# A two-stage layer on one core: unit 0 by pairs of heads, its mixing in whole float32, and an order table in place of due times

## The chip, the cores and the metric

The kernel runs on one core of one Trainium2 chip. The metric is the device time of one execution in microseconds. The core has a matrix engine (PE, with its weight loads listed apart as PEld), three engines for elementwise work (DVE, ACT, POOL), a queue engine that issues most transfers (SP), and 16 DMA engines shared by all queues. SBUF is the on-chip memory of 128 partitions, PSUM the accumulator memory that PE writes.

## The reference

The inputs are q, k, v and a complex decay a (`a_re`, `a_im`), each of 4 batches, 8 heads, 768 steps and 48 columns, in float32, and the parameters of a gated feed-forward stage: `mu_k`, `mu_r` (384), `w_k` (384 x 1024), `w_v` (1024 x 384), `w_r` (384 x 384). For each batch and head a complex 48 x 48 state runs over the steps:

```
scale = min(|a|, 0.999) / (|a| + 1e-6)          # a scaled so that its magnitude stays under one
S     = (a * scale)[:, None] * S + k_t v_t^T    # complex S, real k v^T
y_t   = q_t @ Re(S)
```

The eight heads' y side by side are x (4 batches x 768 steps x 384 columns), and with x_prev the step before:

```
xk = mu_k * x + (1 - mu_k) * x_prev ;  xr = mu_r * x + (1 - mu_r) * x_prev
out = sigmoid(xr @ w_r) * (relu(xk @ w_k)**2 @ w_v)
```

## The kernel before

**Units.** The work is cut into 8 units: a batch and a half of its 768 steps (384 steps). Each unit goes through three phases. A *gate* phase (`gate`, lines 541 to 718) turns a, k and q into rotated keys and queries; an *attention* phase (`attend`, lines 720 to 914) makes y in chunks of 64 steps with a running state; a *mixing* phase (`mix`, lines 336 to 466) is the feed-forward stage.

**Gate.** The state's decay is written as a running sum of logarithms and of angles. ACT takes logarithms, exponentials, arctangents and sines (line 264 is the helper that issues them and loads function tables, line 261); DVE forms the running sums (scans, lines 637 and 665), clips (627, 646, 688), reduces angles (682, 685), takes an absolute value with a bit mask (691), multiplies k and q by the magnitudes (line 654, three instructions of 128 x 768 per unit) and by cosine and sine (line 704, six of them). Rows of the 384 columns lie in three tiles of 128 partitions, in the order of the heads: a head of 48 rows can lie across two tiles. Unit 0's gate is done in two groups, (0, 1) and (1, 3), of these tiles, the others' in one.

**Attention.** `stack` (line 727) copies each head's four parts, cosine and sine, key and query, by SP transfers into tiles `kq` of 112 rows, 20 transfers per unit. `advance` (755) transposes the keys on PE (768), copies them out of PSUM on ACT (774), makes the state's updates on PE (789) and adds them up on DVE (800, six additions of 112 x 384 per unit). `scores` (806) multiplies a head's 112 rows of keys and queries (818), 96 matmuls of 64 columns per unit, and DVE applies the causal mask (823). `values` (830) adds the state's part and the chunk's own part (849). ACT copies y out of PSUM into a tile `ys` (871), and 10 SP transfers per unit (882) carry it into `X`, the input of the mixing.

**Mixing.** PE multiplies in a reduced float32 form (float32r), so every operand is split into a high and a low part and every product is three matmuls: high x high, low x high, high x low (`product`, line 376). DVE makes the difference to the step before (348) and the mixed input (356); ACT rounds the high part (364), DVE subtracts for the low part (367). Nine matmuls of 128 x 384 form one block z; three blocks are the gate r, eight are `first` (line 407: z, relu on ACT 418, square on ACT 422, high part on DVE 426, low part on DVE 430) and eight are `second` (437, o, line 444). A unit's mixing is 171 matmuls. `end` multiplies r with v (460) and stores (463).

**Weights.** They arrive as 64-bit words in ten pieces (`fetch`, 483) and are converted (`convert`, 493): ACT takes an absolute value (506), DVE assembles the bits in four instructions (509, 512, 516, 520), ACT rounds the high part (526) and POOL subtracts for the low part (529). The order of the pieces is `w_r` first, then `w_k` and `w_v` in turn.

**Order.** All engines' instructions are emitted in an order that a planner in the kernel (`Plan`, lines 70 to 239) writes out before: a list schedule, with a cost for each operation, in which each engine takes, of what is ready in that model, the operation with the smallest due time (`due`, 111, worked back from the order of PE). Once emitted, every engine runs its own list in order and waits on semaphores.

## Time and profile before

| | us |
|---|---|
| median of three runs | 477.33 (476.31 to 477.69) |
| the profiled execution | 476.16 |
| its span, first to last instruction | 474.4 |
| PE busy | 382.8 |
| DVE busy | 374.5 |
| ACT busy | 299.9 |
| POOL busy | 32.3 |

Times in profile rows are microseconds from the span's start unless a row says ns. A row of a group names the line, the engine, the operation, out<-in, shapes and count, then busy time and mean ns of one, then the idle time of the engine just before these instructions and what ended it. A row of the timeline has start, length, engine, line and operation. Matmuls are pipelined and their ends are modelled, so that the distance of two starts says more about PE than the length of one. One execution was profiled; the engines not named in a wait may still have been the cause of it.

### The profile page before, as it was taken

What the parts mean: (1) busy time and instruction counts of PE and PEld (TensorE: products, weight loads), DVE (VectorE), ACT (ScalarE), POOL (GpSimd) and SP (SyncE); (2) the same over time, 40 slices, a digit from 0 to 9 for tenths busy, and PEclk for the clock granted to TensorE, in tenths of its full rate; (3) what the DMA queues carried; (4) which work ended last, traced back from release to release, by engine and by line L of the source; (5) the groups of instructions that cost most, each with busy time, mean ns of one, the idle gap of its engine ahead of it and who ended that gap; (6) DMA issues with size and microseconds to landing.
All of it is one profiled execution on the core that took longest, in us unless ns stands there. A gap on an engine that the chain in (4) does not pass through costs nothing.

```text
span 474.4 us, 12425 instructions
## 1 busy us (share of the span) xinstructions
PE 382.8 (81%) x5162; PEld 351.0 (74%) x5162; DVE 374.5 (79%) x610; ACT 299.9 (63%) x498; POOL 32.3 (7%) x45
## 2 busy tenths in 40 slices
PE   0008445879966999979989999999799988999994
PEld 0006433868755999869978898999689967999993
DVE  0798999969989889898989799569967898248222
ACT  7768445597549667957894775866669753434530
POOL 4004210214210000000000000000000000000000
PEclk9999755789978999999999999999899989999998
DMA  8998154502717056416551834072523115210101
GB/s 287 409 409 142 36 184 161 123 1 52 275 26 182 21 195 203 106 51 192 181 130 61 296 102 114 34 252 100 135 78 82 45 48 137 76 35 10 51 0 57
DMA packets 25935, 60.26 MB, mean 127 GB/s; under 512 B 5392, under 2 KB 14608, under 8 KB 25872
## 3 DMA queue, kind: packets, MB, share of 16 engines
q1 hardware_dynamic: 25872, 59.40, 40.7%
q8 instruction: 42, 0.69, 0.6%
q14 instruction: 21, 0.17, 0.1%
HBM read 31.07 MB, written 4.72 MB: 75 GB/s over the span
## 4 chain that ended last, share of the span: by engine, by line
PE 42%; DVE 28%; ACT 13%; DMA 7%; issue 5%; SPq 3%; POOL 1%; DVEq 0%; ACTq 0%
PE z L381 19%; PE o L444 12%; PE y L849 5%; DVE ph L665 4%; DMA kq<-g 3%; PE sc L818 3%; DVE g L654 3%; DMA g<-in_gat 3%; SPq L736 3%; PE up L789 2%; ACT sq L264 2%; DVE m L637 2%; DVE g L704 2%; DVE xm L356 2%; ACT L261 2%
## 5 line engine op out<-in xcount | busy, mean ns | idle before, releaser
L381 PE MATMUL z<-x,w 128*128 128x384 f32 x792 | 155.9, 347 | 5.0 <-DVE state L800 1.9
L381 PEld LDWEIGHTS z<-x,w 128*128 128x128 f32 x792 | 140.3, 193 | 8.4 <-DVE state L800 2.2
L444 PE MATMUL o<-hhi,w 128*128 128x384 f32 x384 | 103.8, 353 | 1.3 <-DVE hhi L426 1.3
L444 PEld LDWEIGHTS o<-hhi,w 128*128 128x128 f32 x384 | 71.3, 196 | 3.2 <-DVE hhi L426 2.5
L444 PE MATMUL o<-hlo,w 128*128 128x384 f32 x192 | 67.9, 354 | 5.6 <-DVE hlo L430 5.5
L768 PE MATMUL tr<-ident,g 128*128 128x128 f32 (+1 forms) x144 | 27.7, 311 | 49.3 <-DVE g L704 47.8
L418 ACT ACTIVATE r<-z 128x384 f32<-128x384 f32 x64 | 31.0, 486 | 55.2 <-PE z L381 55.0
L768 PEld LDWEIGHTS tr<-ident,g 128*128 128x128 f32 (+1 forms) x144 | 17.8, 148 | 55.9 <-issue 31.9
L426 DVE CAST hhi<-h 128x384 fp32r<-128x384 f32 x64 | 22.6, 353 | 33.3 <-ACT h L422 21.2
L704 DVE TENSOR_TENSOR g<-g,r 128x768 f32<-128x768 f32 x48 | 43.7, 951 | 1.8 <-ACT r L264 1.7
L444 PEld LDWEIGHTS o<-hlo,w 128*128 128x128 f32 x192 | 37.8, 197 | 8.7 <-DVE hlo L430 8.6
L818 PE MATMUL sc<-kq 112*64 112x64 f32 x768 | 31.7, 233 | 8.9 <-DMA kq<-g 2.7
L818 PEld LDWEIGHTS sc<-kq 112*64 112x64 f32 x768 | 26.9, 144 | 15.5 <-issue 6.2
L430 DVE TENSOR_TENSOR hlo<-h,hhi 128x384 fp32r<-128x384 f32 x64 | 35.8, 559 | 1.4
L264 ACT ACTIVATE sq<-m 128x1152 f32<-128x1152 f32 (+2 forms) x27 | 28.1, 1054 | 11.1 <-DVE m L620 7.0
L364 ACT CAST x<-xm 128x384 fp32r<-128x384 f32 x48 | 24.2, 511 | 17.1 <-DVE xm L356 13.6
L422 ACT ACTIVATE h<-r 128x384 f32<-128x384 f32 x64 | 33.2, 523 | 2.5 <-DVE hlo L430 1.5
L789 PEld LDWEIGHTS up<-v,kt 64*48 64x48 f32 (+1 forms) x1408 | 27.0, 139 | 6.8 <-ACT kt L774 3.9
L849 PE MATMUL y<-kq,state 112*48 112x64 f32 (+1 forms) x704 | 25.7, 229 | 7.5 <-DVE state L800 5.1
L849 PEld LDWEIGHTS y<-kq,state 112*48 112x48 f32 (+1 forms) x704 | 23.2, 136 | 11.4 <-DVE state L800 5.3
L789 PE MATMUL up<-v,kt 64*48 64x48 f32 (+1 forms) x1408 | 29.4, 231 | 2.4 <-DVE state L800 1.3
L529 POOL TENSOR_TENSOR w<-wx,w 128x768 fp32r<-128x768 f32 (+1 forms) x10 | 24.5, 2454 | 85.6 <-ACT w L526 85.6
(74 smaller groups left out, 551.3 us busy)
## 6 DMA issues: line engine op xcount, KB each, us to landing
kq<-g SPq DMA_DIRECT2D x96, 144.0 KB, 3.2
g<-in_gat SPq DMA_DIRECT2D x18, 768.0 KB, 6.9
raw<-in_w_all SPq DMA_DIRECT2D x9, 768.0 KB, 11.6
g<-in_gat SPq DMA_DIRECT2D x12, 384.0 KB, 7.3
v<-in_vt SPq DMA_DIRECT2D x24, 192.0 KB, 4.6
out_t<-y SPq DMA_DIRECT2D x24, 192.0 KB, 2.1
xt<-ys SPq DMA_DIRECT2D x48, 72.0 KB, 2.2
kq<-g SPq DMA_DIRECT2D x32, 96.0 KB, 2.8
```

Of the source, the lines that this page charges most:

```text
L264: nc.scalar.activation(out=out, in_=in_, func=func, **kw)
L381: nc.tensor.matmul(z, lhsT=wt[s[0]][:, part, s[1]], rhs=r[which][:, ct], start=n == 0, stop=n == 3 * NT - 1)
L418: nc.scalar.activation(out=t["r", j], in_=t["f", j], func=AF.Relu)
L422: nc.scalar.activation(out=t["h", j], in_=t["r", j], func=AF.Square)
L430: nc.vector.tensor_tensor(out=t["lo", j], in0=t["h", j], in1=t["hi", j].bitcast(F32), op=ALU.subtract)
L444: nc.tensor.matmul(tiles["o", mt], lhsT=wt[W_V + 2 * j][:, part, ts(mt, P)], rhs=r, start=j == 0 and n == 0, stop=j == NJ - 1 and n == 2)
L529: nc.gpsimd.tensor_tensor(out=t["w"][:, :, 1], in0=t["x"], in1=t["w"][:, :, 0].bitcast(F32), op=ALU.subtract)
L704: nc.vector.tensor_tensor(out=g[:, ct, 2 * i:2 * i + 2], in0=g[:, ct, 2:4], in1=t["r"][:, ct, 1 - i:2 - i].to_broadcast([P, 2, U]), op=ALU ...
L768: nc.tensor.transpose(out=t["tr", c, part][:, ct * P:(ct + 1) * P], in_=G[u][:, ct, 2 * part, c * P:c * P + rows], identity=ident)
L789: nc.tensor.matmul(t["up", c, s][i * HR:(KR if i else HR), h * D:(h + 1) * D], lhsT=keys[r, i * D:(2 * D if i else HR)], rhs=V[u][c][r, h ...
L818: nc.tensor.matmul(sc[s * SB:s * SB + SB, i, c], lhsT=kq[h][:, 0, q], rhs=kq[h][:, 1, q], start=True, stop=True)
L849: nc.tensor.matmul(t["y", v][s][rows, h // 2 % 2, c], lhsT=lhsT[:, cols], rhs=rhs, start=(s, h % 2) not in begun, stop=stop)
```

## The change

**Pair layout.** The 384 columns are put in another order on the host: tile i of 128 partitions holds the two heads of pair i in partitions 0 to 47 and 64 to 111, and in the remaining 16 + 16 partitions a third of each of heads 6 and 7. Keys of pairs 0 to 2 are read in place for the scores, as two products of 48 rows per head (cosine and sine part) in place of one of 112; heads 6 and 7 are still gathered. Queries for the state's part are copied by SP as before. ACT writes y of pairs 0 to 2 from PSUM straight into X; pair 3 goes through `ys` and six transfers.

**Unit 0 by pairs.** Unit 0's gate is done in three groups of one tile, and its attention pair by pair (`advance_pair`): transposes, updates, 24 state additions of 96 columns, scores and values of one pair need only that pair's tile. The other units work in two teams of two pairs.

**Unit 0's mixing whole.** Its inputs, hidden values and weights stay whole float32 on PE: one matmul per product in place of three, 57 in all, without the splits of lines 364, 367, 426 and 430. Its gate r comes at the end of the mixing, and `w_r` is now the last piece to be converted.

**Weights.** A piece is fetched into buffer i + 1, converted whole into buffer i, and split into buffer i - 1 once unit 0's mixing has used the piece that lies there (`split`: ACT rounds, POOL subtracts). So a conversion waits for the one before, and a split for unit 0's mixing.

**Gates.** The positive part replaces the absolute value and a separate check: one activation less per gate, with the check summed by the exponential. The absolute value of line 691 moves from DVE to ACT. For units 1 to 7, line 654's three instructions and the sine half of line 704's six move to POOL.

**Order.** A table `ORDER` gives each step of each phase a place per engine; it replaces the due times as the planner's choice among ready operations. Some of the planner's costs change, and a tile is counted free 0.16 us later.

```diff
-W_R, W_K, W_V = 0, NT, NT + 1
+W_K, W_V, W_R = 0, 1, 2 * NJ
+ORDER = {
+    ("g", 0): dict(SP=(5, 2, 7, 15, 27, 24, 9, 23, 25,), ACT=(74, 58, 34, ...
...
-R_XK = 2
+R_XK = 1
-GROUPS_0 = ((0, 1), (1, 3))
+POOL_KQ = {u: ((0,1,2), (), (0, 1, 2)) for u in range(1, NU)}
+GROUPS_0 = ((0, 1), (1, 2), (2, 3))
...
-    def due(self):
...
+    def due(self, places):
+        steps = {}
+        for o in self.ops:
+            steps.setdefault((o["key"][0], o["engine"]), set()).add(o["key"][1])
+        place = {}
+        for (phase, e), s in steps.items():
+            given = places.get(phase, {}).get(e, range(len(s)))
+            place.update(((phase, e, x), n) for x, n in zip(sorted(s), given, strict=True))
+        return [place[o["key"][0], o["engine"], o["key"][1]] for o in self.ops]
...
-            for which in (1, 0):
-                sx = slot("x")
+            for which in ((0, 1) if whole else (1, 0)):
+                sx = None if whole else slot("x")
+                def whole_one(which=which):
+                    if which not in hi:
+                        hi[which] = mp["x"].tile([P, NT, 2, U], F32R, tag=("xk", "xr")[which], name="x")[:, :, 0].bitcast(F32)
+                    nc.vector.scalar_tensor_tensor(
+                        out=hi[which][:, ct], in0=d[ct], scalar=mu_sb[:, which, ct:ct + 1],
+                        in1=X[u][:, ct, 0:U], op0=ALU.mult, op1=ALU.add)
...
             for ct, s in enumerate(blocks):
+                if whole:
+                    nc.tensor.matmul(z, lhsT=wx[s[0]][:, s[1]], rhs=hi[which][:, ct], start=ct == 0,
+                                     stop=ct == NT - 1)
+                    continue
...
+                if whole:
+                    parts = (1, tiles["h", j]),
...
+        return steps + gates * whole + [lambda: sigmoid(u)] + [lambda mt=mt: end(mt) for mt in range(NT)]
...
-                raws[i] = keep.tile([P, n, C, 2], I32, tag=f"w{i}", name="raw")
+                raws[i] = keep.tile([P, n, C, 2], I32, tag=f"w{i + 1}", name="raw", padded_shape=[P, PIECE, C, 2])
...
+                t["x"] = whole[i] = keep.tile([P, n, C], F32, tag=f"w{i}", name="wx", padded_shape=[P, 2 * PIECE, C])
...
+            op_act(size, f0, reads=r, writes=[*k, ("raw", i)])
...
+        def split(i):
+            def f0():
+                t["w"] = w = keep.tile([P, 2, n, C], F32R, tag=f"w{(i - 1) % (len(pieces) + 1)}", name="w",
+                                       padded_shape=[P, 2, PIECE, C])
+                wt.update((s.start + k, w[:, :, k]) for k in range(n))
+                nc.scalar.copy(out=w[:, 0], in_=whole[i])
+            def f1():
+                nc.gpsimd.tensor_tensor(out=t["w"][:, 1], in0=whole[i], in1=t["w"][:, 0].bitcast(F32), op=ALU.subtract)
...
+            old = [("wx", j) for j in range(NW)[pieces[i - 1]]] if i else [("raw", len(pieces))]
+            op_act(n * C, f0, reads=k, writes=[("whi", i), *old])
+            op_pool(n * C, f1, reads=[*k, ("whi", i)], writes=[("w", j) for j in blocks])
...
-                    op_dve(2 * U, lambda ct=ct: nc.vector.tensor_tensor(
+                    op_two(2 * U, lambda e, ct=ct: e.tensor_tensor(
                         out=G[u][:, ct, 2:4], in0=G[u][:, ct, 2:4], in1=t["sq"][:, ct], op=ALU.mult),
+                           ct in POOL_KQ.get(u, ((),) * 3)[0], reads=...
...
+                op_act(n, lambda: nc.scalar.activation(out=t["r"][:, 1, c], in_=t["r"][:, 0, c], func=AF.Abs),
...
+                    op_two(2 * U, lambda e, ct=ct: times(e, ct, 1), ct in POOL_KQ.get(u, ((),) * 3)[2], reads=[("r0", u, ct)],
...
+            teams = [(p,) for p in range(NP)] if u == 0 else [(0, 1), (2, 3)]
...
+                            move(lambda i=i, j=j: qs[v][i * HR:i * HR + D, j, a - 2 * v:e - 2 * v],
+                                 lambda i=i, j=j: G[u][j * HR:j * HR + D, a:e, 2 * i + 1], D, e - a, i, cts, cts)
...
+                for n in range(2 * NC):
+                    c, s = divmod(n, 2)
+                    def add(n=n, c=c, s=s):
+                        cols = slice(2 * D * p, 2 * D * p + 2 * D)
+                        new, old = state[(n + 1) % NS][:, cols], state[n % NS][:, cols]
...
+                                    g = G[u][j * HR:j * HR + D, p]
+                                    for i in range(2):
+                                        nc.tensor.matmul(y, lhsT=g[:, 2 * i, q], rhs=g[:, 2 * i + 1, q], start=i == 0,
+                                                         stop=i == 1)
...
+                        if NT not in ps_:
+                            o = X[u][:KR, ps_[0]:ps_[0] + n, 1:U + 1].rearrange(
+                                "p a (c s q) -> p a c s q", s=2, q=SB)[:, :, :, s]
...
+            run(mix(u, u == 0), ("m", u))
+            if u == 0:
+                for i in n:
+                    run([lambda i=i: split(i)], ("s", i))
...
+            plan[0].run(ORDER)
```

More of the change, by code (lines that the diff above doesn't have):

```diff
@@ L64 @@
 ST_X = 0
-ST_SQ, ST_L, ST_PHI = (NP * NU + i * NT * NU for i in range(3))
+ST_SQ, ST_L, ST_PHI = (8 * NU + i * NT * NU for i in range(3))
 ST_RE = ST_PHI + NC * NT * NU
@@ L236, in run @@
                     o["start"], o["end"], o["on"], o["took"] = t, end, e, o["cost"]
-        self.length = end
+        self.length = max(o["end"] for o in ops)
         for i in order:
@@ L314, in tile_kernel @@
     nc.sync.dma_start(out=mu_sb, in_=mu)
-    pieces = [slice(0, 1)] + [slice(i, i + PIECE) for i in range(1, NW, PIECE)]
-    wt = {}
+    pieces = [slice(i, min(i + PIECE, NW)) for i in range(0, NW, PIECE)]
+    wt, wx = {}, {}
     mp = {}
@@ L385, in parts @@
         def parts(which):
-            return [(k, u, which, ct) for k in ("xhi", "xlo") for ct in range(NT)]
+            return [(k, u, which, ct) for k in (("xhi",) if whole else ("xhi", "xlo")) for ct in range(NT)]
+        w_key = "wx" if whole else "w"
+        cost = 1.97 if whole else 1.62
         def gate_r(mt):
@@ L398, in out_ @@
                 nc.scalar.copy(out=zr[u][:, mt], in_=tiles["z", mt])
-            op_pe(1.58, mul, reads=parts(1) + [("w", W_R + ct) for ct in range(NT)], writes=[("z", u, mt)],
+            op_pe(cost, mul, reads=parts(1) + [(w_key, W_R + ct) for ct in range(NT)], writes=[("z", u, mt)],
                   uses=[sp, part_slot[1]])
             op_act(U, out_, psum=True, reads=[("z", u, mt)], writes=[("zr", u, mt)], uses=[sp, zr_slot[u]])
-        steps += [lambda mt=mt: gate_r(mt) for mt in range(NT)]
+        gates = [lambda mt=mt: gate_r(mt) for mt in range(NT)]
+        steps += gates * (not whole)
         so = slot("o")
@@ L407, in first @@
         def first(j):
-            sp, sr, sh, s1, s2 = (slot(t) for t in ("ps", "r", "r", "hhi", "hlo"))
-            hs[j] = s1, s2
+            sp, sr, sh = (slot(t) for t in ("ps", "r", "r"))
+            hs[j] = s1, s2 = (sh, sh) if whole else (slot("hhi"), slot("hlo"))
             t = tiles
@@ L465, in end @@
             op_dma(196, store, reads=[("y", u, mt)], uses=[sr])
-        return steps + [lambda: sigmoid(u)] + [lambda mt=mt: end(mt) for mt in range(NT)]
+        return steps + gates * whole + [lambda: sigmoid(u)] + [lambda mt=mt: end(mt) for mt in range(NT)]
     with ExitStack() as fast:
@@ L479, in tile_kernel @@
         G, g_slot, V, v_slot = {}, {}, {}, {}
-        raws = {}
+        raws, whole = {}, {}
         def fetch(i):
@@ L835, in values @@
+            def values(team):
+                m = len(team)
+                sp = [slot("ps"), slot("ps")]
+                hs = [2 * p + j for p in team for j in range(2)]
                 inter = [n for n in range(2 * NC * half, 2 * NC * (half + 1)) if n]
@@ new lines, in values, with f @@
+                for ps_ in ([team] if NT not in team else [(p,) for p in team[::-1]]):
+                    for s in range(2):
+                        take(s, ps_)
+                if NT in team:
+                    for i in range(NT):
+                        for j in range(2):
+                            def f(i=i, j=j):
+                                o = j * HR + 16 * i
+                                nc.sync.dma_start(out=X[u][j * HR + D:j * HR + HR, i, 1:U + 1],
+                                                  in_=t["ys"][o:o + 16].rearrange("p o c s q -> p (o c s q)"))
+                            op_dma(30, f, reads=[("ys", u, 0), ("ys", u, 1), ("Xy", u, i, 0), ("Xy", u, i, 1)],
+                                   writes=[("Xp", u, i, j)], uses=[sy, x_slot[u]])
```

566 lines of the change are left out of this document (342 added, 224 removed).

## The prediction

> **What bounds the kernel now.** The page's first two lines say that no engine fills the span:
>
> ```profile
> span 474.4 us, 12425 instructions
> PE 382.8 (81%) x5162; PEld 351.0 (74%) x5162; DVE 374.5 (79%) x610; ACT 299.9 (63%) x498; POOL 32.3 (7%) x45
> ```
>
> An average over unlike stages says little, so I looked for the marks between stages: the first mixing matmul of unit 0 (timeline of PE), the first one of unit 1 (chain of waits), and the stages they cut (table by stages: length, busy time of PE, PE's weight loads, DVE, ACT and POOL with instructions, granted clock, DMA share, GB/s).
>
> ```profile
> 88.34 9.58 PE L381 MATMUL z<-x,w 128*128 128x384 f32 x45 [1.90 <-DVE state L800]
> 154.14 1.83 PE z L381 x9
> ...
> 0.00:38.40 38.40, 2.74 (x8) 1.44 (x8) 24.57 (x43) 27.89 (x42) 5.73 (x21) 1.00 0.96 354
> 38.40:88.30 49.90, 27.83 (x641) 23.41 (x641) 48.40 (x67) 26.89 (x44) 9.50 (x5) 0.69 0.48 131
> 88.30:154.10 65.80, 53.70 (x576) 48.01 (x576) 59.32 (x88) 47.21 (x72) 15.20 (x6) 0.87 0.37 106
> 154.10:467.90 313.80, 298.53 (x3937) 278.13 (x3937) 241.66 (x416) 197.93 (x342) 1.89 (x13) 0.99 0.35 104
> 467.90:474.40 6.50, 0.00 (x0) 0.00 (x0) 0.55 (x2) 0.00 (x0) 0.00 (x0) 0.70 0.29 98
> ```
>
> At 38.4 unit 0's gates end (its last rotation, line 704). From there to 154.1, 115.7 us long, DVE is busy 48.40 + 59.32 = 107.7 us, 93% of the time, while PE runs at granted clocks of 0.69 and 0.87. The two stages belong to DVE. From 154.1 to 467.9 PE is busy 298.5 of 313.8 us; that stage belongs to PE, and 15.3 us of idle time are all that a better order can take out of it. Two cycles of it, and the last unit's mixing alone:
>
> ```profile
> 201.40:248.70 47.30, 42.97 (x542) 39.76 (x539) 41.31 (x69) 35.70 (x61) 0.00 (x0) 1.00 0.47 139
> 248.70:296.00 47.30, 45.77 (x661) 42.76 (x662) 44.09 (x78) 29.34 (x53) 0.24 (x1) 1.00 0.48 143
> 437.90:467.90 30.00, 29.95 (x173) 29.35 (x172) 10.49 (x24) 10.63 (x20) 0.00 (x0) 1.00 0.06 21
> ```
>
> So the run is 154.1 us to unit 1's mixing, six cycles of 47.3 us (283.8), 30.0 us of last mixing, and 6.5 us of end. DVE is busy (241.66 - 10.49) / 6 = 38.5 us in a cycle.
>
> **The change, part by part.** I take DVE's work between 38.4 and unit 1's mixing, and ask what of it goes, what comes and what no longer stands there. First the groups of DVE in 38.4 to 88.3, then those in 88.3 to 154.1 (busy us, mean ns).
>
> ```profile
> L367 DVE TENSOR_TENSOR x<-xm,x 128x384 fp32r<-128x384 f32 x6 | 3.3, 550 | 0.0
> L654 DVE TENSOR_TENSOR g<-g,sq 128x768 f32<-128x768 f32 x3 | 2.8, 944 | 0.0
> ...
> L704 DVE TENSOR_TENSOR g<-g,r 128x768 f32<-128x768 f32 x6 | 5.4, 953 | 1.3 <-ACT r L264 1.3
> L430 DVE TENSOR_TENSOR hlo<-h,hhi 128x384 fp32r<-128x384 f32 x8 | 4.8, 606 | 0.0
> L426 DVE CAST hhi<-h 128x384 fp32r<-128x384 f32 x8 | 2.8, 349 | 0.0
> L800 DVE TENSOR_TENSOR state<-up,state 112x384 f32<-112x384 f32 x3 | 1.6, 549 | 0.0
> L691 DVE TENSOR_SCALAR r<-r 128x1152 int32<-128x1152 int32 x1 | 0.9, 946 | 0.0
> L646 DVE TENSOR_SCALAR m<-m 128x1152 f32<-128x1152 f32 x1 | 0.7, 745 | 0.0
> L644 DVE COPY stat<-m 128x3 f32<-128x3 f32 x1 | 0.2, 154 | 0.0
> ```
>
> *Removed.* Unit 0 mixes whole values: its six subtractions of line 367 go (3.3) and its eight pairs of lines 426 and 430 (2.8 + 4.8 = 7.6). The absolute value of line 691 moves to ACT (unit 1's: 0.9). Lines 654 and half of 704 move to POOL for unit 1 (2.8 + 5.4 / 2 = 5.5). Together 17.3 us.
>
> *Added.* Unit 0's pairs need 24 state additions of 96 columns in place of six of 384. No row has that shape: the floor is the tiny copy of line 644 (0.15), the ceiling line 800's 0.55. By the line between them 0.26, so 24 x 0.26 - 6 x 0.55 = 2.9 us; the ends are 0.4 and 9.9.
>
> *No longer in the way.* In the stretch of 88.3 to 154.1 stand also the gates of unit 2: twelve lines of groups, from L704's 5.4 (quoted) to L646's 0.7 (quoted), 27.6 us, with one early instruction of unit 3 in them. Unit 1's mixing needs none of it. Before, mixing 0 was so late that DVE finished it anyway; with mixing 0 early, it falls under mixing 1's 30.0 us of PE and the cycle behind. I take it out, and price the opposite as a rival. If that cover fails it costs 27.6 / 0.93 = 29.7 us.
>
> *The moved work still holds DVE.* The weights' subtraction is the only arithmetic POOL does now. DVE and POOL rows around one of them, and one DVE row from another:
>
> ```profile
> L529 POOL TENSOR_TENSOR w<-wx,w 128x768 fp32r<-128x768 f32 (+1 forms) x10 | 24.5, 2454 | 85.6 <-ACT w L526 85.6
> ...
> 107.97 1.96 DVE L627 TENSOR_SCALAR m<-m 128x1152 f32<-128x1152 f32 x1
> 115.56 4.38 POOL L529 TENSOR_TENSOR w<-wx,w 128x768 fp32r<-128x768 f32 x1 [6.24 <-ACT w L526]
> 117.29 0.95 DVE L520 SCALAR_TENSOR_TENSOR wx<-raw,wx 128x768 int32<-128x768 int32 x1
> 118.63 2.13 DVE L654 TENSOR_TENSOR g<-g,sq 128x768 f32<-128x768 f32 x1
> 131.35 1.83 POOL L529 TENSOR_TENSOR w<-wx,w 128x768 fp32r<-128x768 f32 x1 [6.26 <-ACT w L526]
> ```
>
> Line 654 takes 0.94 when undisturbed and 2.13 here: 1.2 us lost, its end (120.76) just behind POOL's (119.94). Before that line 520 ran at its usual length while POOL's 1.83 became 4.38. So either waits, and DVE loses about 1.2 us per POOL instruction; the ends are nothing and 1.83. Unit 1's six cost DVE 7.2 us (0 to 11.0); the ten of the weights are in the old sum already.
>
> The Trainium skill (SBUF — State Buffer, "Who interferes with whom") states that a DVE instruction with two SBUF inputs and a GpSimd one that reads SBUF exclude each other, and the second blocks fully until the first ends. The trace agrees with a wait of this kind on both sides. By the rule's worst case the move costs 11.0 in place of 7.2, and unit 1's mixing comes 4.1 us later.
>
> *The sum.* 107.7 - 27.6 - 17.3 + 2.9 + 7.2 = 72.9 us of DVE. At the same 93% that is 78.3 us behind 38.4: unit 1's mixing begins near 116.7 in place of 154.1, a gain of 37.4 us.
>
> *Whole float32 on PE.* 57 matmuls replace 171 in mixing 0. No row shows this shape whole. Neighbouring starts on the timeline of PE:
>
> ```profile
> 158.74 1.14 PE L789 MATMUL up<-v,kt 64*64 64x48 f32 x64
> 159.80 1.84 PE L381 MATMUL z<-x,w 128*128 128x384 f32 x9
> 161.57 0.92 PE L818 MATMUL sc<-kq 112*64 112x64 f32 x24
> 162.42 3.39 PE L381 MATMUL z<-x,w 128*128 128x384 f32 x18
> ```
>
> The split z takes 29.95 / 173 = 0.173 us each in the last stage, the floor. The whole-float32 scores take (162.42 - 161.57) / 24 = 0.035, two in the array at once, so 0.071 per 64 columns and 0.43 per 384; the updates (1.06 / 64 = 0.0166, four at once, 48 columns) give 0.53, the ceiling. Mixing 0 is 9.9 to 30.2 us; I take 0.43, 24.5 us. When it begins follows from DVE too (groups of 38.4 to 88.3):
>
> ```profile
> L356 DVE SCALAR_TENSOR_TENSOR xm<-dx,mu_sb,xt 128x384 f32<-128x384 f32 x6 | 3.6, 614 | 0.1
> L823 DVE TENSOR_TENSOR pt<-sc,mask 128x384 f32<-128x384 f32 x4 | 2.2, 539 | 0.0
> L348 DVE TENSOR_TENSOR dx<-xt 128x384 f32<-128x384 f32 x3 | 1.7, 553 | 0.1
> ```
>
> These and the additions (6.2) are 13.7 us; with one conversion and the landing of pair 3 some 20 us behind 38.4, so near 60. From 60 to 116.7 mixing 0 and attention 1 (13 to 16 us, a quoted cycle's PE less the last mixing's 30) have 56 us for at most 46. PE lies under DVE's conversions and gates 1 and adds nothing; without that cover the whole form is 24.5 - 30.0 = -5.5 us against the split one. The Trainium skill (FP8 and Floating Point Precision, "TensorE Precision Notes") states four passes for true float32: 4 x 0.173 x 57 = 39.4 us by the page, which just fits.
>
> *Scores per unit.* Each head of a pair takes two products of 48 rows, so 168 matmuls for 96. At 0.0166 for the 144 that can share the array four ways and 0.035 for 24 it is 3.2 us against 3.4 now: nothing. If all of them cost 0.035 it is 5.9, 15 us over six cycles.
>
> *DMA, SP, ACT.* Queries still go over SP, keys are read in place, and three pairs of y are written to X by ACT itself. Per unit SP issues 20 kq transfers before and after (24 in unit 0) and 6 of y for 10:
>
> ```profile
> kq<-g SPq DMA_DIRECT2D x96, 144.0 KB, 3.2
> xt<-ys SPq DMA_DIRECT2D x48, 72.0 KB, 2.2
> ```
>
> The 2.2 us of landing stay, for pair 3's pieces. The early loads are merely in another order; DMA is 0.96 busy up to 38.4 either way, and weights are converted in order behind that. A conversion now waits for the one before (its buffer holds the last raw piece); it is DVE work already counted. ACT loses one activation per gate and gains one, loses unit 0's six casts, and gains six key copies per unit, each at most this row's 0.48:
>
> ```profile
> L774 ACT COPY kt<-tr 128x384 f32<-128x384 f32 (+1 forms) x48 | 21.3, 478 | 11.6 <-PE tr L768 11.6
> ```
>
> At 47.21 of 65.8 us ACT has room for that; were ACT the bound, it would be 2.9 us per unit. POOL's queue is in order: behind a weight split, which waits for mixing 0 to be done with the buffer it overwrites, stand the gates' POOL instructions, and behind those the transposes.
>
> *Cycles.* DVE sheds 5.7 + 0.9 and pays 7.2 for the lock, so it stays at 39 of 47.3. I leave the six cycles as they are, with 15 us to gain.
>
> Span 474.4 - 37.4 = 437.0. The profiled execution took 476.16 us, 1.8 over its span, so 438.8; the median shown is 477.33, 1.2 above that execution. I forecast **440 us**.
>
> **The rivals.** *PE's idle goes too* (0.20). With DVE lighter and X landing sooner the 15.3 us of idle PE shrink to nothing: 425. For it: the idle is scattered over short waits. Against: the lock gives DVE's relief back.
>
> *Gates 2 are not covered, or the order does not pull unit 0 forward* (0.16). Then DVE must finish them before it gets on, as now: 440 + 29.7 = 470. For it: DVE was the bound and still has the same conversions. Against: mixing 1 is 30 us of PE in which it needs only 7.6 us of DVE for its own splits.
>
> *Slower: the gates' chain through POOL* (0.06). Three instructions of 2.45 in place of 0.94, twice in a row, make a gate 9.0 us longer. If every cycle waits for its gate, units 1 to 7 pay 7 x 9.0 = 63: 503. It decides from 37.4 / 7 = 5.3 us per unit that come through. The waits of PE in 154 to 440 speak against it, with only 2.7 us on the rotation in three waits:
>
> ```profile
> PE tr L768 <- DVE g L704: 2.7, 3, 1.7
> ```
>
> **How the numbers follow.** The forecast has 0.56, with its own range of 428 to 454 (state additions at their ends, the lock at 0 or 1.83, scores at 0.035). The rivals have 0.20, 0.16 and 0.06, and 0.02 is left for no difference, where 0.3% is about what can be told. Faster is 0.56 + 0.20 + 0.16 = 0.92. For 8 in 10 the range goes from 416, below the second case, to 468, near the third.
>
> **What would show it.** Right: unit 1's first z at 110 to 125; no DVE rows for lines 367, 426, 430 of unit 0; DVE near 90% busy up to that mark; cycles near 47. Wrong: unit 1's z first after 140 (gates 2 in the way), PE waiting on POOL before transposes by more than 5 us per unit, or mixing 0 itself bound by PE from its first z to its last.

## The result and the profile after

| kernel | median, us | range, us | ratio to before, 95% interval |
|---|---|---|---|
| before, beside it | 477.51 | 476.31 to 477.97 | |
| after | 495.71 | 493.47 to 496.84 | 1.0379 [1.0338, 1.0421] |

The changed kernel is 3.8% slower, where 440 us was forecast. Its profiled execution took 495.93 us, 2.0 over its span.

The busy times on after's page, with a span of 493.9 us and 13531 instructions:

```profile
PE 392.5 (79%) x5681; PEld 345.7 (70%) x5681; DVE 385.6 (78%) x568; ACT 308.9 (63%) x591; POOL 118.3 (24%) x82
```

DVE has 42 instructions less than before (568 for 610), and 11.1 us more of busy time (385.6 for 374.5). POOL went from 32.3 to 118.3 us.

After's stages, as a table by stages with the columns of the prediction. The marks are the end of unit 0's gates (33.0), the first whole z of unit 0 (74.7), the first split z of unit 1 (153.5) and PE's last product (487.4):

```profile
33.00:74.70 41.70, 17.68 (x502) 15.26 (x496) 30.97 (x61) 21.86 (x42) 6.54 (x4) 0.71 0.43 132
74.70:153.50 78.80, 66.38 (x894) 44.31 (x894) 74.49 (x90) 53.65 (x97) 26.49 (x12) 0.89 0.27 76
153.50:487.40 333.90, 305.12 (x4240) 283.55 (x4233) 257.43 (x375) 208.88 (x400) 80.32 (x50) 0.96 0.26 76
```

Unit 0's mixing begins 13.6 us sooner than before (74.7 for 88.3), but unit 1's begins at the same time (153.5 for 154.1). Behind that mark the run takes 333.9 us for 313.8. So two things need an explanation: where the sooner start went, and what costs 20 us in the stage of PE.

The groups of DVE, first of before, then of after (busy us, mean ns), for the same three operations:

```profile
L704 DVE TENSOR_TENSOR g<-g,r 128x768 f32<-128x768 f32 x48 | 43.7, 951 | 1.8 <-ACT r L264 1.7
L430 DVE TENSOR_TENSOR hlo<-h,hhi 128x384 fp32r<-128x384 f32 x64 | 35.8, 559 | 1.4
...
L426 DVE CAST hhi<-h 128x384 fp32r<-128x384 f32 x64 | 22.6, 353 | 33.3 <-ACT h L422 21.2 <-PE o L444 12.1
```

```profile
L508 DVE TENSOR_TENSOR hlo<-h,hhi 128x384 fp32r<-128x384 f32 x56 | 44.2, 791 | 2.3
L504 DVE CAST hhi<-h 128x384 fp32r<-128x384 f32 x56 | 34.6, 619 | 39.2 <-ACT h L497 22.7 <-PE o L529 14.5 <-PE up L891 1.9
L790 DVE TENSOR_TENSOR g<-g,r 128x768 f32<-128x768 f32 x27 | 34.2, 1311 | 5.2 <-ACT r L322 5.2
```

The counts fell as the change says, the mean lengths rose by 42%, 75% and 38%. And PE waits for just these. Its waits behind unit 1's first z, of before and then of after:

```profile
PE tr L768 <- DVE g L704: 2.7, 3, 1.7
...
PE o L444 <- DVE hlo L430: 1.8, 2, 1.1
...
PE o L444 <- DVE hhi L426: 1.1, 3, 0.6
```

```profile
PE tr L862 <- DVE g L790: 14.2, 7, 4.2
PE o L529 <- DVE hlo L508: 6.8, 7, 1.9
PE o L529 <- DVE hhi L504: 2.6, 3, 1.2
```

These are 23.6 us for 5.6 (us in total, times, longest). For POOL itself PE waits behind this mark once, for 1.1 us. How a wait for DVE comes about stands in the timelines of POOL and DVE:

```profile
PE sc L1005 <- POOL g L790: 1.1, 1, 1.1
...
135.08 4.42 POOL L790 TENSOR_TENSOR g<-g,r 128x768 f32<-128x768 f32 x2 [5.09 <-ACT r L322]
...
137.76 2.56 DVE L790 TENSOR_TENSOR g<-g,r 128x768 f32<-128x768 f32 x1
```

DVE's rotation takes 2.56 us where it took 0.95 before, and ends at 140.3, just behind POOL's two products (139.5). PE, ahead of unit 1's first z here, has waited 4.24 us for it when it goes on at 140.4.

### The profile page after: what moved, and what is told of

Read it like the earlier page. It is cut to its first block, busy times and chain, and to the rows that moved or that the text cites. A ratio compares the mean times of both kernels' runs of the same rounds, so it can differ in the third digit from the quotient of the medians.

```text
span 493.9 us, 13531 instructions
## 1 busy us (share of the span) xinstructions
PE 392.5 (79%) x5681; PEld 345.7 (70%) x5681; DVE 385.6 (78%) x568; ACT 308.9 (63%) x591; POOL 118.3 (24%) x82
## 4 chain that ended last, share of the span: by engine, by line
PE 44%; DVE 33%; ACT 12%; issue 6%; SPq 2%; DMA 1%; DVEq 0%; ACTq 0%
PE z L452 15%; PE o L529 13%; PE y L1042 5%; DVE g L790 5%; DVE ph L752 5%; PE up L891 4%; DVE hhi L504 4%; DVE hlo L508 3%; PE sc L1005 2%; PE tr L862 2%; SPq L820 2%; ACT sq L322 2%; DVE dx L404 2%; DVE x L430 2%; DVE wx L601 1%
## 5 line engine op out<-in xcount | busy, mean ns | idle before, releaser
L452 PE MATMUL z<-x,w 128*128 128x384 f32 x693 | 134.4, 344 | 0.5 <-ACT zr L472 0.3
L452 PEld LDWEIGHTS z<-x,w 128*128 128x128 f32 x693 | 121.6, 191 | 2.1 <-DVE x L430 0.5
L741 POOL TENSOR_TENSOR g<-g,sq 128x768 f32<-128x768 f32 x21 | 42.5, 2048 | 180.9 <-ACT sq L322 122.3
L790 POOL TENSOR_TENSOR g<-g,r 128x768 f32<-128x768 f32 x21 | 46.5, 2237 | 76.4 <-ACT r L322 63.8
L430 DVE TENSOR_TENSOR x<-xm,x 128x384 fp32r<-128x384 f32 x42 | 31.6, 764 | 10.8 <-ACT x L427 10.7
L790 DVE TENSOR_TENSOR g<-g,r 128x768 f32<-128x768 f32 x27 | 34.2, 1311 | 5.2 <-ACT r L322 5.2
L448 PE MATMUL z<-x,wx 128*128 128x384 f32 x66 | 24.6, 519 | 17.3 <-DVE x L413 15.8
L322 ACT ACTIVATE sq<-m 128x1152 f32<-128x1152 f32 (+1 forms) x30 | 28.2, 966 | 8.5 <-DVE m L733 5.1
L448 PEld LDWEIGHTS z<-x,wx 128*128 128x128 f32 x66 | 12.8, 202 | 26.1 <-issue 16.7
L891 PEld LDWEIGHTS up<-v,kt 64*64 64x64 f32 (+1 forms) x1216 | 22.3, 131 | 11.6 <-issue 3.9
L1042 PE MATMUL y<-q,state 112*48 112x64 f32 (+1 forms) x704 | 25.9, 228 | 5.6 <-DMA q<-g 5.6
```

The costliest lines, as they stand in the source:

```text
L322: nc.scalar.activation(out=out, in_=in_, func=func, **kw)
L430: e.tensor_tensor(out=lo[which][:, ct], in0=xm[which, ct], in1=hi[which][:, ct].bitcast(F32), op=ALU.subtract)
L448: nc.tensor.matmul(z, lhsT=wx[s[0]][:, s[1]], rhs=hi[which][:, ct], start=ct == 0, stop=ct == NT - 1)
L452: nc.tensor.matmul(z, lhsT=wt[s[0]][:, part, s[1]], rhs=r[which][:, ct], start=n == 0, stop=n == 3 * NT - 1)
L741: op_two(2 * U, lambda e, ct=ct: e.tensor_tensor(out=G[u][:, ct, 2:4], in0=G[u][:, ct, 2:4], in1=t["sq"][:, ct], op=ALU.mult), ct in POOL_ ...
L790: e.tensor_tensor(out=g[:, ct, 2 * i:2 * i + 2], in0=g[:, ct, 2:4], in1=t["r"][:, 1 - i, ct:ct + 1].to_broadcast([P, 2, U]), op=ALU.mult)
```

## The experiments

Every comparison is with runs of the kernel before on the same chip, whose median was 476.2 to 476.7 us.

### Without POOL's products, and with them alone

The first kernel takes POOL's products out of after. The second is the kernel before with nothing changed but POOL's products. The third keeps them for unit 1 alone.

```diff
-POOL_KQ = {u: ((0,1,2), (), (0, 1, 2)) for u in range(1, NU)}
+POOL_KQ = {}
```

> The kernel after with the 42 gate products of units 1 to 7 back on DVE; everything else stays. Theory A (exclusion): a POOL product holds an SBUF path that DVE's instructions need, and DVE pays for it at instructions that PE waits for. In the kernel after the casts for the hidden values take 619 ns for 353 before, the subtractions 791 for 559, the rotations left on DVE 1311 for 951. With the products back these return to 353, 559 and 951; DVE gets 42 x 0.95 = 40 us of work back and loses some 57 us of waiting, and the time is 465 to 482. Theory B (length of the gate chain through POOL): three products of 2.0 to 2.2 us in place of 0.95, twice per unit, are 7 us per unit late; then the time falls by 30 to 50 us, to 445 to 465, and the long DVE rows are only a symptom. Theory C (the order table or the rest of the change): the time stays at 490 to 500.

```diff
-                    op_dve(2 * U, lambda ct=ct: nc.vector.tensor_tensor(
+                    op_two(2 * U, lambda e, ct=ct: e.tensor_tensor(
...
+                           u > 0, reads=[("sq0", u, ct), ("sq1", u, ct)], writes=[("g", u, ct, 2), ("g", u, ct, 3)],
...
+                    op_two(2 * U, lambda e, ct=ct: times(e, ct, 1), u > 0, reads=[("r0", u, ct)],
```

> The kernel before with one part of the change alone: the magnitude products and the sine half of the rotation of units 1 to 7 on POOL. Theory A (exclusion): DVE sheds 40 us and waits 57 us, at instructions that PE waits for: 485 to 500 us, and the same DVE rows (cast, subtraction, rotation) grow as in the kernel after. Theory B (chain length): 7 us per unit more, 500 to 525 us. Theory C (the move is harmless, the rest of the change is at fault): 470 to 480 us.

```diff
-POOL_KQ = {u: ((0,1,2), (), (0, 1, 2)) for u in range(1, NU)}
+POOL_KQ = {1: ((0, 1, 2), (), (0, 1, 2))}
```

> The kernel after with the products on POOL for unit 1 only, units 2 to 7 on DVE. It tells the start from the cycles. If the loss is spread evenly over units (theory A in the cycles), the time is near that of the run without any POOL products plus a seventh of the difference (2 to 4 us). If the early stage is what the exclusion spoils (conversions of the weights waiting for POOL while unit 0 mixes), most of the difference is still there.

Measured: after without them 480.27 us (477.79 to 481.19), ratio 1.0093 [1.0059, 1.0126]; before with them 494.72 us (492.98 to 495.64), ratio 1.0396 [1.0363, 1.0429]; for unit 1 alone 483.45 us (482.81 to 484.84), ratio 1.0157 [1.0123, 1.0191].

The first kernel's busy times and the groups of DVE:

```profile
PE 387.5 (81%) x5681; PEld 341.1 (72%) x5681; DVE 358.1 (75%) x610; ACT 308.2 (65%) x591; POOL 26.5 (6%) x40
```

```profile
L790 DVE TENSOR_TENSOR g<-g,r 128x768 f32<-128x768 f32 x48 | 48.6, 1063 | 6.6 <-ACT r L322 6.6
L508 DVE TENSOR_TENSOR hlo<-h,hhi 128x384 fp32r<-128x384 f32 x56 | 30.9, 554 | 2.1
...
L504 DVE CAST hhi<-h 128x384 fp32r<-128x384 f32 x56 | 21.1, 376 | 47.0 <-PE o L529 30.4 <-ACT h L497 16.4
```

The lengths are back (554 and 376 ns), the rotation's nearly (1063 for 951), and with 42 products more DVE is busy 27.5 us less. POOL's products cost after some 14 us (18.2 over the before beside it, 4.0 without them) and the kernel before 18. All three times lie in the ranges of theory A. PE's waits for the three operations behind unit 1's first z are 9.6 us in the first kernel, where after has 23.6, and 21.9 in the second, where before has 5.6. Unit 1's six products cost 3.2 us, so most of the loss comes with the later units' products and not at the start. But 4.0 us over before remain without them: the rest of the change gains nothing either, in this order.

### What of POOL's work costs: its reading or its length

Each of POOL's products is replaced by two fills of the same 128 x 768 elements on POOL. This leaves the products out; POOL still writes where it wrote, but reads nothing.

```diff
+            def fill(ct):
+                for value in (0.05, 0.1):
+                    nc.gpsimd.memset(G[u][:, ct, 2:4], value)
...
-                    op_two(2 * U, lambda e, ct=ct: e.tensor_tensor(
+                    op_two(2 * U, lambda e, ct=ct: fill(ct) if e is nc.gpsimd else e.tensor_tensor(
```

> The kernel after with each of the 42 POOL products replaced by two fills of the same 128 x 768 output on POOL, which write but read nothing. It leaves out the products, so the result is not the layer's; what is compared is time. Theory A with reads: DVE's subtractions and rotations (two inputs from SBUF) return to their short length (559 and 951 ns), and the time falls to 455 to 480. Theory A with any POOL access: they stay at 791 and 1311, and the time stays near 490. Theory B (chain length): the POOL steps last nearly as long, so the time stays near 485 to 495 although the DVE rows are short. The Trainium skill (SBUF - State Buffer, Who interferes with whom) states that a GpSimd instruction that only writes does not hold up a DVE instruction with two SBUF inputs, but does one in a two-port mode; by it the subtractions come back to 559 ns and the cast stays long.

Measured: 446.66 us (445.09 to 447.27), ratio 0.9385 [0.9357, 0.9413], 49 us under after. Its groups of POOL and of DVE:

```profile
L720 POOL MEMSET g<- 128x768 f32 x84 | 63.8, 780 | 156.7 <-DVE g L796 129.5 <-DMA g<-in_gat 24.8
```

```profile
L508 DVE TENSOR_TENSOR hlo<-h,hhi 128x384 fp32r<-128x384 f32 x56 | 32.5, 582 | 2.3
L504 DVE CAST hhi<-h 128x384 fp32r<-128x384 f32 x56 | 26.0, 464 | 43.9 <-ACT h L497 24.4 <-PE o L529 17.6 <-PE up L897 1.9
L796 DVE TENSOR_TENSOR g<-g,r 128x768 f32<-128x768 f32 x27 | 24.6, 955 | 3.8 <-ACT r L322 3.7
```

The time lies under both theories' ranges. The 49 us are not the price of the lock alone. The 42 products are on no engine in this kernel. The chain through POOL is shorter too: a step is 1.56 us for 2.0 to 2.2, and POOL doesn't wait for ACT any more (63.8 us of such waits in after, for the rotation alone). So the run's time doesn't tell the long rows from a long chain. The two runs before it do, which lie outside theory B's ranges (480.27 for 445 to 465, 494.72 for 500 to 525), and so do after's waits: 1.1 us of PE for POOL against 23.6 for the lengthened rows of DVE. What the fills show is which rows the reading lengthens. Operations of DVE with two inputs are back at their length (582 and 955 ns for 791 and 1311); the cast, with one input, is only part of the way back (464 for 619 and 353). The Trainium skill (SBUF — State Buffer, "Who interferes with whom") says the same of both: an instruction of GpSimd that only writes doesn't hold a DVE instruction with two SBUF inputs, and a DVE instruction in a two-port mode, which casts can enter, contends with GpSimd whatever that does.

### The order

Without POOL's products the table still gave 480. In the next two kernels POOL has none either. One goes back to the order of the kernel before, by due times. The other keeps the table's form but has other places in it: they were found by many small exchanges, judged by the planner's own model with all gate products on DVE and its costs nearer to the measured ones.

```diff
-ORDER = {
...
-            run(attend(u), ("a", u))
-            run(mix(u, u == 0), ("m", u))
+            run(attend(u), t + AT_A[0], t + AT_A[1])
+            a, e = AT_M if u else AT_M0
+            run(mix(u, u == 0), t + a, t + e)
```

> Every gate product is on DVE, as in the run without POOL's products (480.27 us), and the order table is taken out: the kernel before's rule orders the work again (due times, attention of unit u at u + 0.2 to u + 0.8, its mixing at u + 1.2 to u + 2.1). Theory 1: the table was made for POOL's products and is what lengthens the stage behind unit 1's first z (325 us without POOL's products against 313.8 before). Then that stage is 305 to 316 us, and the run 455 to 468. Theory 2: the pair layout itself costs this (24 more score products, 96-column additions, six key copies more per unit). Then the stage stays at 320 to 328 and the run at 474 to 484, whatever the order. Unit 1's first z is at 138 to 150 by both.

```diff
-    ("w", 0): dict(ACT=(141,), DVE=(151,)),
...
+    ('w', 0): dict(ACT=(52,), DVE=(88,)),
...
-        plan[0].op("ACT", (0.05 if psum else 0.09) + n / 1200, f, **kw)
+        plan[0].op("ACT", 1.1 * ((0.05 if psum else 0.09) + n / 1200), f, **kw)
...
-        plan[0].op("DVE", 0.07 + n / (960 * rate), f, **kw)
+        plan[0].op("DVE", 1.08 * (0.07 + n / (960 * rate)), f, **kw)
```

> As the run without POOL's products, with another table: the same steps, in another order on each engine, worked out for all gate products on DVE. If the order is what loses, as theory 1 of the run by due times says, this is at 440 to 460 us, with unit 1's first z at 138 to 146 and a stage of 295 to 308 behind it. If the pair layout itself costs (theory 2), it stays at 470 or more. If PE's needs are the floor, DVE's busy time stays at 355 to 360 us and only the waits of PE shrink, from 19 us behind the first z to under 8.

Measured: by due times 450.84 us (450.55 to 450.89), ratio 0.9449 [0.9424, 0.9474]; with the other table 438.38 us (437.63 to 438.90), ratio 0.9184 [0.9158, 0.9210]. The second beats both kernels, by 8.2% and 11.6%. Both times lie a little under the ranges expected (455 to 468, 440 to 460), and theory 2, that the pair layout itself costs, is out: the stage behind unit 1's first z is 296.6 us by due times and 291.2 with the table, not 320 to 328. The groups of work are the same as in the run of 480 us, with the same DVE busy time (354.9 for 358.1). So after's table costs 29 us against the old rule when POOL has no products.

The other table's stages, from the first whole z to the first split one, and from there to PE's last product:

```profile
76.20:139.80 63.60, 61.55 (x894) 41.04 (x894) 56.39 (x79) 52.15 (x96) 12.04 (x6) 0.95 0.38 106
...
139.80:431.00 291.20, 289.79 (x4233) 275.11 (x4233) 232.58 (x403) 204.16 (x396) 10.86 (x17) 1.00 0.29 85
```

Of the 15.3 us of PE's idle time that the prediction saw in the kernel before, 1.4 are left, at a granted clock of 1.00. Now PE is busy nearly throughout both stages, in the first 61.55 of 63.6 us.

Then POOL's products were put into the kernel by due times:

```diff
-POOL_KQ = {}
+POOL_KQ = {u: ((0,1,2), (), (0, 1, 2)) for u in range(1, NU)}
```

> As the run by due times (450.84 us), with the gates' products of line 741 and half of 790 of units 1 to 7 back on POOL. It asks whether the lock costs the same where PE, not DVE, sets most of the time. Theory 1: DVE's rows lengthen again by about 1.35 us for each POOL instruction (hhi over 0.53, rotation over 1.2 us), DVE's busy time rises in place of falling, and the run is 464 to 485. Theory 2: the loss came from the table in after, and with due times POOL relieves DVE: 440 to 451.

Measured: 499.29 us (498.24 to 501.12), ratio 1.0483 [1.0444, 1.0521], above the range of the first theory (464 to 485). Groups of DVE, first by due times without, then with POOL's products:

```profile
L452 DVE TENSOR_TENSOR hlo<-h,hhi 128x384 fp32r<-128x384 f32 x56 | 30.9, 552 | 1.4
...
L448 DVE CAST hhi<-h 128x384 fp32r<-128x384 f32 x56 | 20.3, 362 | 32.6 <-ACT h L441 17.6 <-PE o L473 14.7
```

```profile
L452 DVE TENSOR_TENSOR hlo<-h,hhi 128x384 fp32r<-128x384 f32 x56 | 38.2, 682 | 1.9 <-PE o L473 0.5
...
L448 DVE CAST hhi<-h 128x384 fp32r<-128x384 f32 x56 | 29.2, 524 | 39.4 <-ACT h L441 26.9 <-PE o L473 12.3
```

In this kernel, where PE is busy 381.9 of 449.1 us without them, the same products cost 48 us; the rotation, not shown, goes from 1019 to 1375 ns. After's table takes back 3.6 of them (495.7 for 499.3): it suits POOL's products and costs 29 without them. Of the 47.3 us by which the span grows, 10.1 lie ahead of unit 1's first split z (156.1 for 146.0) and 37.4 behind it (334.0 for 296.6). There PE's waits for hlo, hhi and the rotation go from 1.4 to 24.3 us, and DVE's busy time over the whole span rises by 16 (355.7 to 372.0). Why it is 48 here and 14 to 18 elsewhere stays open beyond that.

### Where the sooner start went

The table of the run without POOL's products was changed in four places only: conversions and splits of the weights first on their engines, gates and attention of unit 2 given places behind.

```diff
-    ("g", 2): dict(SP=(70, 74, 73, 62, 38, 75,), ACT=(152, 59, 153, 148, 113,), DVE=(110, 152, 87, 147, 150,), POOL=(19,
-         15,)),
...
-    ("w", 0): dict(ACT=(141,), DVE=(151,)),
...
+    ('g', 2): dict(ACT=(210, 119, 212, 205, 169,), DVE=(165, 211, 143, 204, 208,), SP=(70, 74, 73, 62, 38, 75,)),
...
+    ('w', 0): dict(ACT=(16,), DVE=(9,)),
```

> As the run without POOL's products, with the table changed in four places: the ten conversions of the weights and the ten splits come ahead of everything else that is ready on their engines, the gates and the attention of unit 2 behind. It tells where the predicted 37 us of the start went. Theory 3 (mine from the prediction): only DVE's load ahead of unit 1's mixing counts, so with gates 2 (27.6 us) behind it the first split z falls from 144.9 to 115 to 128. Theory 4: mixing 0 is held by its own chain (x of unit 0, ReLU, square and the products in turn, the buffers of a weight piece free only when mixing 0 is done with them), so the conversions end 20 to 35 us sooner, near 90 in place of 121.1, but the last whole product and the first split z stay within 8 us of where they are (137 to 153). The run as a whole says little, since the later units are not ordered for it: 475 to 505.

Measured: 499.89 us (498.52 to 501.27), ratio 1.0479 [1.0430, 1.0528]. PE's timeline has the first whole z, the last whole o and the first split z; DVE's has the last conversion:

```profile
80.11 7.17 PE L419 MATMUL z<-x,wx 128*128 128x384 f32 x12 [16.28 <-DVE x L384]
...
154.60 2.20 PE L500 MATMUL o<-h,wx 128*128 128x384 f32 x6
...
162.60 2.67 PE L423 MATMUL z<-x,w 128*128 128x384 f32 x14 [1.89 <-DVE state L872]
```

```profile
90.71 0.56 DVE L576 SCALAR_TENSOR_TENSOR wx<-raw,wx 128x384 int32<-128x384 int32 x1
```

The conversions end at 91.3 in place of 121.1, as theory 4 had it (near 90), and the first split z comes at 162.6, later than either theory said (115 to 128, 137 to 153). Conversions ahead of the rest do not bring unit 1 forward: mixing 0 still runs from 80 to 157. The run does not show the start without gates 2, though. The table gave them later places only, and an engine still takes, of what is ready, whatever has the smallest place: DVE did unit 2's rotations from 132 to 142 and PE its scores from 137 on, both ahead of unit 1's first split z.

What fills most of it is PE, busy 54.9 of 56.8 us from 80.1 to 136.9. Two of three whole products of every z are left out in the next kernel, in the order of 438.38 us.

```diff
-                    nc.tensor.matmul(z, lhsT=wx[s[0]][:, s[1]], rhs=hi[which][:, ct], start=ct == 0,
-                                     stop=ct == NT - 1)
+                    if ct == NT - 1:
+                        nc.tensor.matmul(z, lhsT=wx[s[0]][:, s[1]], rhs=hi[which][:, ct], start=True, stop=True)
```

> As the run with the table worked out for gate products on DVE (438.38 us), with two of the three whole products of every z of unit 0's mixing left out (it leaves out 22 of unit 0's 57 whole float32 products; what remains waits for the last input block and the same weight pieces). There the profile shows 114 whole records for 57 products, 0.345 us each, so a product is 0.69 us and those left out are 15.2 us of PE. Theory 1: PE sets the stage from the first whole z to the first split one (61.55 of 63.6 us busy), so the first split z comes 6 to 15 us sooner, up to where DVE's 56.4 us of that stage end, and the run is 425 to 433. Theory 2, the prediction's: PE lies under DVE's conversions and gates, so nothing moves by more than 2 us: 436 to 440.

Measured: 436.94 us (436.70 to 438.50), ratio 0.9172 [0.9139, 0.9205], 1.4 us under the 438.38; the intervals of the two overlap. That is theory 2's range (436 to 440) and not theory 1's (425 to 433), and the first split z comes 2.1 us sooner (137.7 for 139.8), not 6 to 15. PE's timeline in this kernel:

```profile
111.73 0.81 PE L420 MATMUL z<-x,wx 128*128 128x384 f32 x2
118.83 4.21 PE L500 MATMUL o<-h,wx 128*128 128x384 f32 x6 [6.29 <-ACT h L468]
...
123.75 3.00 PE L976 MATMUL sc<-g 48*64 48x64 f32 x94 [0.31 <-DVE g L761]
...
137.70 1.84 PE L423 MATMUL z<-x,w 128*128 128x384 f32 x9 [0.44 <-ACT kt L843]
```

PE is ahead by 8.9 us at 112.5 (121.4 with all products), and gives 6.8 of it back: it waits 6.3 us for a hidden value, and the scores of unit 2 behind run slowly: 94 in 3.00 us, where 96 take 1.77 at the full clock. The granted clock from 119.0 to 127.0 is 0.50; with all products it is 1.00 from 111.6 to 121.4. Over the stage, here from 76.5 to 137.0, it is 0.80 where the kernel with all products had 0.95:

```profile
76.50:137.00 60.50, 51.75 (x849) 35.78 (x847) 55.92 (x74) 49.45 (x91) 12.06 (x6) 0.80 0.39 107
```
ACT's timeline shows what the hidden value waits for: ahead of it in the queue stands the angle of unit 2, which waits for DVE.

```profile
114.53 1.16 ACT L749 ACTIVATE r<-r 128x1152 f32<-128x1152 f32 x1 [3.76 <-DVE r L746]
...
118.26 0.51 ACT L468 ACTIVATE h<-r 128x384 f32<-128x384 f32 x1
```

So two limits lie close together in this stage: PE's whole products, and the gates of unit 2 with what is queued behind them. Taking some 14 us of products (22 of 0.645 us, as worked out below) from the first alone gives 2 us of start. What both together would give wasn't tried.

### What unit 0's whole float32 form is worth

In the kernel by due times, and in one with a table made for it, unit 0's mixing was put back to split weights and inputs (buffers of the weights as before):

```diff
-            run(mix(u, u == 0), t + a, t + e)
-            if u == 0:
-                run([lambda i=i: split(i) for i in n], 0, 0)
+            run(mix(u), t + a, t + e)
```

> As the run by due times with all gate products on DVE, and unit 0's mixing undone: split weights and split inputs in unit 0 as in the kernel before, the weights split by POOL right behind their conversion, the weight of the receptance first. It prices the whole float32 mixing by itself, under one rule of order. By the terms of the prediction the whole form takes 3.3 + 7.6 us of DVE out of the start, and PE has room: this run is 6 to 14 us slower than the one by due times. The rival: the conversions and the chain of unit 0 set the start either way, so the two are within 3 us; or the splits, which wait in the whole form for the last conversion, cost as much as is saved, and this run is up to 6 us faster.

> As the run with unit 0's mixing split (453.34 us), with a table worked out for it in the same manner as in the run of 438.38 us. It asks if the whole float32 form of unit 0 is worth something once the order is made for each form. By PE's busy time the split form is 57 x 0.69 - 171 x 0.173 = 9.7 us cheaper; by DVE's it is 10.9 us dearer. If the whole form pays because DVE sets the time to the first z, this run is 441 to 448; if PE's 9.7 us decide, 428 to 437.

Measured: by due times 453.34 us (452.24 to 453.76), ratio 0.9495 [0.9466, 0.9524], 2.5 us slower than the whole form; with a table 449.43 us (448.80 to 449.55), ratio 0.9420 [0.9391, 0.9450], 11.0 us slower. The first is what the rival said (within 3 us) and not the 6 to 14 expected; the second lies just above the 441 to 448 that DVE's time would give, and far from the 428 to 437 that PE's would. The page of the second has PE at 368.6 us where the whole form has 377.5, and DVE at 363.0 for 354.9. So the whole form pays although PE is busy 9 us longer with it. That DVE's time is the dearer one at the start fits this, but no run shows it alone.

Read as steps of one change, from the kernel before: the pair layout, unit 0 by pairs and the gates' new steps under the old rule, 476.7 to 453.3; whole unit 0, to 450.8; POOL's products, to 499.3; the table, to 495.7. The first step, which the prediction priced at nearly nothing, is the only large gain along this path. It brings the first z forward from 154.1 to 145.0 and shortens the stage behind from 313.8 to 300.6 us. It was not taken apart; two differences of it are in the groups of DVE, of before and then of the split form by due times: the angle's conversion went from 1347 to 755 ns, and the absolute value of line 691 left DVE.

```profile
L682 DVE TENSOR_SCALAR r<-ph 128x1152 int32<-128x1152 f32 x7 | 9.4, 1347 | 0.1
...
L691 DVE TENSOR_SCALAR r<-r 128x1152 int32<-128x1152 int32 x7 | 6.6, 949 | 0.0
```

```profile
L705 DVE TENSOR_SCALAR r<-ph 128x1152 int32<-128x1152 f32 x7 | 5.3, 755 | 0.0
```

These are (1347 - 755 + 949) x 7 = 10.8 us of DVE, of 13.3 that it is busy less (361.2 for 374.5). The conversion now writes its angle tile with the two halves one behind the other (`[P, 2, NT, U]` for `[P, NT, 2, U]`), a difference that the list of the change does not name; no run changes that alone, so that it shortens the conversion is not shown. What else gained the rest stays open.

## Why the prediction was wrong, step by step

**What bounds the kernel now.** The reading holds: DVE up to unit 1's mixing, PE behind it with 15.3 us to gain. The rival that PE's idle goes came true (1.4 us left) once POOL was left alone and the order made for it.

**Removed, Added.** The counts and sizes are right: 8 hhi and 8 hlo less, 42 subtractions of x for 48. The additions of 96 columns took 0.253 us where 0.26 was taken (the line between the two rows gives 0.25). In the groups of DVE from 33 to 74.7, and in the timelines of PE and ACT:

```profile
L974 DVE TENSOR_TENSOR state<-up,state 112x96 f32<-112x96 f32 x20 | 4.6, 253 | 0.6 <-DVE state L974 0.2
...
58.11 0.82 PE L1042 MATMUL y<-pt,v 64*64 64x64 f32 x24
...
64.41 0.31 ACT L1077 ACTIVATE ys<-y 112x192 f32<-112x192 f32 x1
...
74.72 5.59 PE L448 MATMUL z<-x,wx 128*128 128x384 f32 x12 [15.79 <-DVE x L413]
```

The lower rows show what the sum left out, the way from the last y to the first x. PE is done with unit 0's attention at 58.9 and then waits 15.8 us: ACT copies pair 3's y only at 64.4, behind steps of unit 1's gates in its queue, its six transfers are issued from 65.2 to 68.8, and DVE's first difference stands at 72.3. So the first whole z came at 74.7 and not near 60. DVE was busy 31.0 of these 41.7 us; the 93% of the long stage didn't hold here.

**The moved work still holds DVE.** The mechanism is right, and the size close. DVE's busy time without 42 products of 0.952 us would have been 318.1 in the run without POOL's products, 315.7 by due times and 334.5 in the kernel before; with them on POOL it was 385.6, 372.0 and 395.0. That is 1.61, 1.34 and 1.44 us of DVE for each product, where 1.2 was taken and 1.83 was the upper end. More than 0.952 means that the move is a loss on DVE itself. The working already had that: 7.2 paid for 5.5 shed.

**Cycles.** Of the 56.9 us that the span lies over the sum (493.9 for 437.0), 20.1 are in the stage behind unit 1's first z (333.9 for 313.8), and this step, the overlap of the lock with PE, is what failed there. "DVE sheds 5.7 + 0.9 and pays 7.2 for the lock, so it stays at 39 of 47.3" treated the lock as a load in a stage where DVE has room. But it falls on hhi, hlo and the rotation, for which PE waits: 23.6 us of waits for 5.6. DVE's busy share in a cycle doesn't show which of its instructions PE is queued behind. POOL's products cost the whole run 14 to 48 us, by the order.

**No longer in the way.** This failed too. The other 36.8 us lie ahead of unit 1's first z (153.5 for 116.7): besides this step, the late first whole z (14.7), the whole products, and the lock are in them, the last with some 9 (the mark is at 144.9 without POOL's products). Between 33.0 and 153.5 DVE is busy 30.97 + 74.49 = 105.5 us where the sum had 72.9. After still does the gates of units 1 and 2 in full there, as the two instances of each of their rows of 1152 columns show, here one of them:

```profile
L707 DVE SCALAR_TENSOR_TENSOR m<-sq,m 128x1152 f32<-128x1152 f32 x2 | 2.7, 1354 | 0.3 <-ACT sq L322 0.3
```

And after mixing 0 PE's own order puts attention 2 ahead of unit 1's first z, in after's timeline of PE:

```profile
140.38 1.11 PE L862 MATMUL tr<-ident,g 128*128 128x128 f32 x4 [4.24 <-DVE g L790]
141.42 3.00 PE L1005 MATMUL sc<-g 48*64 48x64 f32 x96
...
153.55 0.62 PE L452 MATMUL z<-x,w 128*128 128x384 f32 x2
```

The rival "gates 2 are not covered" named this, with 470. The order made for the purpose (438 us) keeps gates 2 there as well. Whether a start without them would be sooner stays open: no run has one.

**Whole float32 on PE.** The size was wrong. A step of three products has six records in the timeline, and in after's groups of PE from 74.7 to 153.5 the 57 products have 114:

```profile
L448 PE MATMUL z<-x,wx 128*128 128x384 f32 x66 | 24.6, 519 | 17.3 <-DVE x L413 15.8 <-DVE wx L605 1.5
L529 PE MATMUL o<-h,wx 128*128 128x384 f32 x48 | 18.4, 530 | 3.4 <-ACT h L497 3.4
```

They are 43.0 us, in part at a lowered clock. The records overlap, so their lengths say too much (the 0.69 us in two of the expectations came from them). The distance of two starts says it better, here in the order of 438 us, at a granted clock of 1.00:

```profile
111.67 4.03 PE L419 MATMUL z<-x,wx 128*128 128x384 f32 x12
115.54 4.03 PE L500 MATMUL o<-h,wx 128*128 128x384 f32 x12
```

That is 3.87 us for six products, 0.645 us for one, and 36.8 us for the 57, where I had 24.5. I took 0.43, from two rows of small matmuls that share the array in a way the large ones don't, and called 0.53 the ceiling. With 13 to 16 us of attention 1 the 36.8 would still fit in the 56 of the sum. But the stage also holds some 7 us of attention 2 and runs in part at a lowered clock (0.95 in the mean), and so PE is busy 61.55 of its 63.6 us even in the best order: it doesn't lie under DVE. The Trainium skill (FP8 and Floating Point Precision, "TensorE Precision Notes") states four passes for true float32, which by the split product's 0.173 us is an estimate of 0.69. The trace comes near it, with 0.645. The prediction had this beside it as 39.4 us and called it a case that just fits.

**Scores, DMA, ACT.** Right as far as they were priced: the scores of 48 rows take 1.77 us for 96, and no SP or ACT limit appears outside unit 0's chain by pairs and ACT's queue behind gates 2.

**The sum.** 116.7 was forecast for unit 1's first z; the best run has 139.8. Of these 23.1 us, 16.2 are the first whole z (76.2 for near 60) and 6.9 the stage behind it (63.6 for 56.7). That the best order still comes to 438 us, close to the forecast 440, is luck and no support for the sum: there the start gains 14 us, and the cycles 22.6, which I had left as they were.

**The rivals.** "Slower: the gates' chain through POOL" had the sign and not the mechanism: of its own sign, more than 5 us per unit of PE waiting for POOL, after has 1.1 us in all. Not the steps on POOL cost most, but what they do to DVE.

## What to carry to other kernels

Before work goes from DVE to POOL, compare what DVE sheds per instruction (here 0.95 us) with what POOL's reading costs it (here 1.34 to 1.61 us), and look at which DVE instructions PE waits for: a lock is paid there, not in the average. An order fitted to one set of costs has to be made again when the work moves; here the same work ran at 480, 451 and 438 us in three orders. When a price has no row, take small matmuls that share the array only as a lower bound (they gave 0.43 us here, where 0.645 was measured), and read the price from the distance of starts as soon as there is a row of the right type and size.

## What the runs showed of the hardware

- A product of 128 x 768 elements on POOL costs DVE 1.34 to 1.61 us beside it, and itself takes 2.0 to 2.2 us, where the shortest one took 1.82. A fill of the same size takes 0.78 us and costs two-input instructions of DVE little (hlo 582 ns for 554), but a cast of 376 ns goes to 464.
- A whole float32 product of 128 x 128 by 384 shows as two records and takes 0.645 us from start to start at a granted clock of 1.00, 3.7 times the 0.173 us of a split one.
- In the kernel with two of three whole products left out, PE waited 6.3 us for a hidden value. In the stretch behind that, from 119.0 to 127.0, the granted clock was 0.50, and 94 scores took 3.00 us, where 96 take 1.77 at 1.00.
